# Spectral filter and mixture of experts on one core: small matmuls of the routing placed behind a count or a sum instead of in places of their own

## The chip, the core and the metric

The kernel runs on one core of a Trainium2 chip. Five engines work side by side, each through its own instructions in order: PE (TensorE, matrix products), DVE (VectorE), ACT (ScalarE), POOL (GpSimd, which here issues the indirect DMAs) and SP (SyncE, which issues direct DMAs). The metric is the device time of one execution in microseconds (us), less is better.

## The reference

```python
def _attn_ref(x, filt_r, filt_i):          # x: 8 x 2496 x 256
    X = np.fft.rfft(x, axis=1)
    F = (filt_r + 1j * filt_i)[None, :, :]
    return np.fft.irfft(X * F, n=x.shape[1], axis=1).astype(np.float32)

def _moe_ref(x, w_gate, w1, w2):           # x: 19968 x 256, 8 experts
    cap = N // E                           # 2496 tokens for each expert
    logits = x @ w_gate
    order = np.argsort(-logits.flatten())
...
    for idx in order:
        tok, e = (int(idx) // E, int(idx) % E)
        if assigned[tok] >= 0 or counts[e] >= cap:
            continue
        assigned[tok] = e
        counts[e] += 1
...
    for e in range(E):
        mask = assigned == e
        h = np.maximum(x[mask] @ w1[e], 0.0)
        out[mask] = h @ w2[e]
```

A filter along the sequence by Fourier transforms, then a two-layer network with eight experts. Tokens go to experts greedily, by falling score; an expert that is full takes no more. Every expert ends with exactly 2496 tokens.

## The kernel before

The first 420 us or so hold the Fourier transforms (class `Fft`); their result goes to DRAM as `xs`, and the scores to an array `lg` on chip. The rest is the two-layer network (`Ffn`, the FFN) for one expert slot after the other, with the routing (`Route`) of the next slot woven in.

**The network.** `Ffn.run` takes an expert's 2496 tokens in five tiles of 512 (the last 448). For tile g, `gather` (L819) issues four indirect DMAs on POOL that fetch 128 token rows each into `xg`, by the indices `xid`. `turn` (L826) transposes two of these pieces with four small matmuls (`ptr`, L837), and ACT and DVE copy them as a high and a low part into `xo` and `z`; two turns, half 0 and half 1, make a tile. `first` (L851) does one of eight blocks f of the first layer: six products of 512 columns (`pz`, L859), then ACT and DVE make the high and low part of the result `hl`. The second layer runs by quarters t of a tile: 24 products of 256 columns (`py`, L902), an ACT copy, and a scatter by POOL (L913) to the rows `oid` of the output. `firsts` (L872) yields the blocks, and places the turns of the next tile at blocks 3 and 5 (`TF`), and the gather of the tile after it at block 5. Tile 0 of the next expert is turned by the hook in the last tile's second layer (L1040).

**The search.** For each slot `Route.phase` prepares (L635 to L649: the best open expert of each token, big DVE operations), then searches a score threshold in 11 rounds (`threshold`, L575). A round is a *count* (`counts`, L538: DVE compares all scores with several thresholds, 11 or 13 small 16-bit matmuls at L559 count them, DVE folds the result) and a *sum* (L572: one 16-bit matmul over all partitions), from which DVE makes the next thresholds.

**The look-ups.** When a slot's token set is known, `places` (L745) finds, tile by tile, the rows to fetch and to write. For each tile DVE compares (`GE`, L762), PE runs two *pairs* of 16-bit matmuls (`pr`, L769), ACT counts with a sign function (L773), and DVE ends with `xid` (L779) and `oid` (L786).

**What sets the order.** PE's order is the order in which the program is written (`manual_schedule`); that of DVE, ACT and POOL is made by the framework's scheduler. The class `Pump` writes the routing in between: after each piece of FFN work, `feed(c)` adds the piece's estimated time to a clock. It then steps the look-ups (`side`) if their due time has come, and the search (`main`) while its own has; a step is what stands between two `yield`s, and its kind and size give the next due time by the table `lag`. As long as tile 0 of a slot has no indices, the search stands still (`first`). `until` steps until a tile has its indices; `gather` calls it.

Of the kernel before, what the change touches and what calls it, by code (L numbers as in the profile page):

```python
# [6 lines left out]

F32, F32R = mybir.dt.float32, mybir.dt.float32r
BF, F16, I32 = mybir.dt.bfloat16, mybir.dt.float16, mybir.dt.int32
# [6 lines left out]
G = 22  # L16
# [8 lines left out]
ORD, TF = (1, 0, 0, 1), (3, 5)  # L25
# [108 lines left out]
class Fft:  # L134


    def __init__(s, tc, i, xs, zd, lg, pp):
        s.tc, s.nc, s.i, s.xs, s.zd, s.lg, s.pp = tc, tc.nc, i, xs, zd, lg, pp
        s.zw = s.zo = s.y7 = s.y9 = None
        s.xos = []  # L140
        s.nload = s.nstore = 0
        s.st_x = tc.nc.sync
        s.cps = tc.nc.vector.tensor_copy, tc.nc.scalar.copy
        s.y1c = {}
        s.Y1, s.yt, s.yd, s.z, s.xr, s.vs = {}, {}, {}, {}, {}, {}
# [644 lines left out]
class Ffn:  # L790
# [52 lines left out]
    def run(s, e, pump, hook):  # L843
# [7 lines left out]
        def first(g, f):  # L851
            n = min(512, CAP - 512*g)
            xh, xl = s.xT[e, g]
            p = s.ps.tile([128, 512], F32, name="pz", tag="c", bufs=4)
            m = 0
            for k in range(2):
                sl = slice(1024*k+128*f, 1024*k+128*f+128)
                for w, x in ((w1h, xh), (w1h, xl), (w1l, xh)):
                    nc.tensor.matmul(p[:, :n], w[:, sl], x[:, k, :n], start=m == 0, stop=m == 5)  # L859
                    m += 1  # L860
                yield 0.65 * n / 512
            hl = s.wp.tile([128, 1024], F32R, name="hl", bufs=NH)
            hs.setdefault(g, []).append(hl)
            h, l = (hl[:, 512*k:512*k+512] for k in range(2))
            s.lasta = s.R.relu = nc.scalar.activation(h[:, :n], p[:, :n], AF.Relu).ins  # L865
            if g < 4:
                s.R.low = nc.vector.scalar_tensor_tensor(l[:, :n], p[:, :n], 0.0, h[:, :n].bitcast(F32), op0=OP.max, op1=OP.subtract).ins  # L867
            else:
                for a, b, c in ((384, n, n), (0, 384, 512)):
                    s.R.low = nc.vector.scalar_tensor_tensor(hl[:, c:c+b-a], p[:, a:b], 0.0, h[:, a:b].bitcast(F32), op0=OP.max, op1=OP.subtract).ins  # L870

        def firsts(g, count):  # L872
            for f in range(len(hs.get(g, ())), min(8, len(hs.get(g, ())) + count)):
                if g + 1 < 5:
                    if f == TF[0]:
                        s.turn(e, g + 1, 0)
                    if f == TF[1]:
                        s.turn(e, g + 1, 1)
                        if g + 2 < 5:
                            hook(('g', g + 2))  # L880
                yield from first(g, f)

        hook(('g', 1))
        for g in range(5):
            n = min(512, CAP - 512*g)
            yield from firsts(g, 8)
            if g == 4:
                hook('last')
            if g == 0:
                hook('w2')  # L890
            for t in range(4):
                if g < 4:
                    yield from firsts(g + 1, ORD[t])
# [5 lines left out]
                m = 0  # L899
# [24 lines left out]
def emit(tc, i, out):  # L924
    nc = tc.nc
    with ExitStack() as st:
# [9 lines left out]
        f = Fft(tc, i, xs, zd, lg.rearrange("p (b g) e -> p b g e", g=G), pp)  # L936
# [21 lines left out]
        W = None  # L958
# [19 lines left out]
        pump = Pump(R)  # L978
# [30 lines left out]
        def gather(e, g):  # L1009
            pump.until((e, g))  # L1010
            W.gather(e, g, pump.out[e])
# [11 lines left out]
        def flush(p):  # L1023
            while split and split[0][1] < p:
                with tc.issue_after(W.lasta):
                    W.split(*split.pop(0))
        with tc.manual_schedule(engines={mybir.EngineType.PE}):
            for e in range(8):
                pump.limit = e + 1
                def hook(what):  # L1030
                    if what == 'w2':
                        flush(8)
                    elif isinstance(what, tuple):
                        gather(e, what[1])
                    elif e < 7:
                        if what == 'last':
                            gather(e + 1, 0)
                            flush(4)
                        else:
                            W.turn(e + 1, 0, what - 1)  # L1040
                for pe in W.run(e, pump, hook):
                    pump.feed(pe)
                    n += 1

                    if split and n % PACE == 0:
                        with tc.issue_after(W.lasta):
                            W.split(*split.pop(0))


class Pump:  # L1050
# [3 lines left out]
    def __init__(s, R):  # L1054
        s.R, s.ph, s.tags, s.out, s.limit, s.clock = R, 0, set(), {}, 0, 0.0
        s.main, s.due, s.held = R.phase(0), 0.0, False
        s.side = []
        s.on_w, s.kind = None, ''
        s.lag = dict(d=lambda t: t, G=lambda n: LAGS[s.ph][0] + 0.17 * n, X=lambda n: LAGS[s.ph][1], m=lambda t: 1.0 + 1.2*t, w=lambda t: t,
                     o=lambda t: t, p=lambda t: t, g=lambda t: 3.0)  # L1060

    def step_main(s):
        if s.held:
            if s.ph > s.limit:
                return False
            s.held = False
            tab, BE, widx = s.R.made
            xid, oid = (s.R.wb.tile([128, 20], I32, name=n, bufs=2) for n in ("xid", "oid"))
            s.out[s.ph] = (xid, oid, widx)
            s.side.append([s.clock, s.ph, s.R.places(s.ph, tab, BE, xid, oid)])  # L1070
            s.on_w(s.ph)
            return True
        if s.main is None:
            return False
        y = next(s.main, None)
        if y is None:
            s.ph += 1
            s.main = s.R.phase(s.ph) if s.ph < 8 else None
            return s.main is not None
        k, t = y  # L1080
        s.kind = k
        s.held = k == 'w'
        s.due = s.clock + s.lag[k](t)
        return True
# [5 lines left out]
    def step_side(s, u):  # L1090
        y = next(u[2], None)
        if y is None:
            s.side.remove(u)
            return
        k, t = y
        if k == 'g':
            s.tags.add((u[1], t))
        u[0] = s.clock + s.lag[k](t)

    def feed(s, c):  # L1100
        s.clock += c
        for u in s.side[:1]:
            if u[0] <= s.clock:
                s.step_side(u)
        while s.due <= s.clock and not s.first() and s.step_main():
            pass

    def until(s, tag):
        while tag not in s.tags:
# [23 lines left out]
```

## Time and profile before

| | before |
|---|---|
| median of 3 runs | 1418.15 us (1418.12 to 1419.26) |
| the profiled execution's own time | 1418.68 us |
| its span | 1416.9 us |
| PE busy | 1377.6 us, 97% |
| DVE busy | 891.2 us, 63% |
| ACT busy | 674.6 us, 48% |
| POOL busy | 485.5 us, 34% |
| mean granted clock of PE | 0.989 |

The profile is one execution recorded by the hardware. The span runs from the first to the last instruction; the 1.8 us beside it are start and end. An engine counts as busy while one of its instructions runs; matmuls overlap, so the distance between the starts of two of them tells more than the duration of one. The granted clock is PE's share of full speed: 1.00 is 2.4 GHz, 0.50 is 1.2 GHz.

### The profile page before, as it was taken

The numbers are of one execution on the slowest core, as the hardware profiler recorded it, in microseconds if no ns is written. First come the engines' busy times: TensorE is split into PE (matmuls) and PEld (weight loads), VectorE is DVE, ScalarE is ACT, GpSimd is POOL, SyncE is SP. The second block draws the span as 40 slices with busy tenths as digits, with TensorE's granted clock in tenths as the row PEclk, the third lists the DMA queues.
The fourth block names the chain that finished last, engine by engine and source line by source line (L and its number), as shares of the span: only waits on it lengthen the run. The fifth ranks groups of instructions, "written<-read, shape, count | busy, mean of one in ns | idle before, by whom it ended". The sixth has DMA issues, their size and how long they took to land.

```text
span 1416.9 us, 27230 instructions
## 1 busy us (share of the span) xinstructions
PE 1377.6 (97%) x10338; PEld 1209.3 (85%) x10338; DVE 891.2 (63%) x2548; ACT 674.6 (48%) x1638; POOL 485.5 (34%) x538
## 2 busy tenths in 40 slices
PE   9999999999969999999999999999999999999998
PEld 8998898876437898898888889888898999899988
DVE  5577676775547768668667876876967635423231
ACT  6766666644564346326335534533623635423231
POOL 3343343431023126324421732433334324323312
PEclk9999999999979999999999999999999999999999
DMA  9786675658981022102212212112111321111100
GB/s 374 262 237 184 191 217 137 160 125 239 319 311 57 29 83 70 40 27 97 63 36 75 73 44 83 53 47 99 46 39 49 127 68 51 48 41 51 40 20 29
DMA packets 58700, 153.75 MB, mean 109 GB/s; under 512 B 10953, under 2 KB 32073, under 8 KB 54985
## 3 DMA queue, kind: packets, MB, share of 16 engines
q1 hardware_dynamic: 29920, 70.10, 16.4%
q0 software_dynamic: 18416, 60.37, 13.0%
q10 hardware_dynamic: 10233, 21.53, 4.6%
q8 instruction: 82, 1.34, 0.4%
q14 instruction: 49, 0.40, 0.1%
HBM read 88.32 MB, written 63.70 MB: 107 GB/s over the span
## 4 chain that ended last, share of the span: by engine, by line
PE 58%; issue 5%; DVE 5%; POOL 1%; ACT 1%; DMA 0%; POOLq 0%; DVEq 0%; ACTq 0%
PE py L902 28%; PE pz L859 25%; PE ptr L837 2%; PE rt L559 2%; POOL out L913 1%; PE rt L769 1%; DVE hl L870 1%; DVE w1l L817 1%; DMA wr<-w,widx 0%; DVE tmp L640 0%; DVE Gm L551 0%; DVE hl L867 0%; ACT junka L773 0%; DVE tmp L638 0%; DVE M L636 0%
## 5 line engine op out<-in xcount | busy, mean ns | idle before, releaser
L902 PE MATMUL py<-w1h,hl 128*128 128x256 f32 x2496 | 483.8, 286 | 0.7 <-DVE hl L870 0.7
L902 PEld LDWEIGHTS py<-w1h,hl 128*128 128x128 f32 x2496 | 401.7, 191 | 3.3 <-DVE hl L870 1.1
L902 PE MATMUL py<-w1l,hl 128*128 128x256 f32 (+1 forms) x1280 | 358.8, 282 | 0.0
L913 POOL DMA_INDIRECT out<-y,oid x160 | 167.2, 1045 | 495.8 <-ACT y L912 448.2
L865 ACT ACTIVATE hl<-pz 128x512 fp32r<-128x512 f32 (+1 forms) x320 | 188.0, 588 | 229.6 <-PE pz L859 203.9
L859 PE MATMUL pz<-xo,w0h 128*128 128x512 f32 (+1 forms) x640 | 264.1, 413 | 3.9 <-DVE hl L867 2.1
L867 DVE SCALAR_TENSOR_TENSOR hl<-pz,hl 128x512 fp32r<-128x512 f32 x256 | 175.3, 688 | 135.4 <-ACT hl L865 134.1
L859 PE MATMUL pz<-z,w0h 128*128 128x512 f32 (+1 forms) x640 | 248.6, 388 | 0.0
L859 PE MATMUL pz<-xo,w0l 128*128 128x512 f32 (+1 forms) x640 | 248.4, 388 | 0.0
L902 PEld LDWEIGHTS py<-w1l,hl 128*128 128x128 f32 (+1 forms) x1280 | 241.0, 188 | 1.9
L823 POOL DMA_INDIRECT xg<-xs,xid x160 | 170.6, 1067 | 135.3 <-issue 50.6
L912 ACT COPY y<-py 128x256 f32<-128x256 f32 x152 | 56.6, 372 | 298.7 <-PE py L902 269.5
L859 PEld LDWEIGHTS pz<-xo,w0l 128*128 128x128 f32 x640 | 120.8, 189 | 24.1
L859 PEld LDWEIGHTS pz<-xo,w0h 128*128 128x128 f32 x640 | 121.6, 190 | 22.4 <-DVE hl L867 3.3
L859 PEld LDWEIGHTS pz<-z,w0h 128*128 128x128 f32 x640 | 121.6, 190 | 15.7 <-DVE z L841 0.6
L219 ACT COPY Y<-p 64x240 f32<-64x240 f32 (+1 forms) x302 | 115.3, 382 | 28.6 <-PE p L213 21.1
L237 POOL TENSOR_TENSOR P<-P 128x256 f32<-128x256 f32 x80 | 58.7, 733 | 166.5 <-DVE P L235 166.3
L551 DVE TENSOR_TENSOR Gm<-M,thr 117x1232 bf16<-117x1232 f32 (+2 forms) x80 | 104.4, 1315 | 0.2
L213 PE MATMUL p<-cS,xr 117*128 117x120 f32 x688 | 93.5, 276 | 2.7 <-ACT Y L219 1.5
L213 PEld LDWEIGHTS p<-cS,xr 117*128 117x128 f32 x688 | 85.1, 191 | 6.8 <-ACT Y L219 4.3
L229 PE MATMUL p<-cW,Y 128*128 128x128 f32 x640 | 88.8, 277 | 0.6 <-DVE Q L236 0.6
L229 PEld LDWEIGHTS p<-cW,Y 128*128 128x128 f32 x640 | 80.1, 191 | 5.8 <-issue 3.9
(218 smaller groups left out, 1989.2 us busy)
## 6 DMA issues: line engine op xcount, KB each, us to landing
z<-zd SPq DMA_DIRECT2D x26, 600.0 KB, 5.2
zd<-zt SPq DMA_DIRECT2D x120, 128.0 KB, 3.3
xs<-xo ACTq DMA_DIRECT2D x18, 600.0 KB, 9.8
xr<-x SPq DMA_DIRECT2D x6, 1536.0 KB
xr<-x SPq DMA_DIRECT2D x6, 1216.0 KB, 11.5
zd<-zt ACTq DMA_DIRECT2D x40, 128.0 KB, 2.6
xs<-xo SPq DMA_DIRECT2D x8, 600.0 KB, 6.2
xr<-x SPq DMA_DIRECT2D x8, 512.0 KB, 6.8
```

Of the source, the lines that this page charges most:

```text
L213: s.lastmm = nc.tensor.matmul(p[:, q-q0, :120], xv[:, q-24*h], s.cS1, start=True, stop=True).ins
L219: c = (nc.vector.tensor_copy if (t == 5 if b else cp) else nc.scalar.copy)(dst, src)
L229: nc.tensor.matmul(p[:, k], s.Y1[b][:, 4*g+k, dh*128:dh*128+128], s.cW[:, 4*g+k], start=True, stop=True)
L237: nc.gpsimd.tensor_tensor(P[:, :, :64], P[:, :, :64], P[:, :, 64:], op=OP.subtract)
L551: nc.vector.tensor_tensor(Gm[:, s0:s1, :m], s.M[:, s0:s1].unsqueeze(2).to_broadcast([117, s1 - s0, m]), thr[:117].unsqueeze(1).to_broadcas ...
L823: s.lastg = s.nc.gpsimd.indirect_dma_start(out=xg[:n], out_offset=None, in_=s.xs, in_offset=bass.IndirectOffsetOnAxis(ap=ids[0][:n, t:t+1] ...
L859: nc.tensor.matmul(p[:, :n], w[:, sl], x[:, k, :n], start=m == 0, stop=m == 5)
L865: s.lasta = s.R.relu = nc.scalar.activation(h[:, :n], p[:, :n], AF.Relu).ins
L867: s.R.low = nc.vector.scalar_tensor_tensor(l[:, :n], p[:, :n], 0.0, h[:, :n].bitcast(F32), op0=OP.max, op1=OP.subtract).ins
L902: nc.tensor.matmul(p[:a.stop-a.start], hs[g][f][:, a], b[:, 256*f:256*f+256], start=m == 0, stop=m == 8 * len(terms) - 1, skip_group_check ...
L912: s.lasta = nc.scalar.copy(y, p).ins
L913: st = nc.gpsimd.indirect_dma_start(out=out_rows, out_offset=bass.IndirectOffsetOnAxis(ap=ids[1][:w, 4*g+t:4*g+t+1], axis=0), in_=y[:w], i ...
```

## The change

`firsts` no longer writes a turn into PE's order itself: at blocks 0 and 3 it puts the turn on a list `turns`, and `flush` writes what is still on the list at blocks 3 and 6. So does the hook for tile 0 of the next expert, with a `flush` before the next expert begins. `feed` first steps the search; if one of the steps was a count, a sum or the end of the search (`'G'`, `'X'`, `'m'`), that is a `hit`: one turn of the list is written directly behind it, and then `beside` may write a look-up step behind that. Without a hit, `beside` writes no look-up as long as the search or its preparation runs (`soon`), but for the step behind a finished tile (`'g'`).

```diff
@@ firsts
                 if g + 1 < 5:
-                    if f == TF[0]:
-                        s.turn(e, g + 1, 0)
+                    if f in (0, 3):
+                        pump.flush()
+                        pump.turns.append(partial(s.turn, e, g + 1, f // 3))
+                    if f == 6:
+                        pump.flush()
                     if f == TF[1]:
-                        s.turn(e, g + 1, 1)
                         if g + 2 < 5:
                             hook(('g', g + 2))
@@ hook
                         else:
-                            W.turn(e + 1, 0, what - 1)
+                            pump.flush()
+                            pump.turns.append(partial(W.turn, e + 1, 0, what - 1))
+                pump.flush()
                 for pe in W.run(e, pump, hook):
@@ Pump
-            s.side.append([s.clock, s.ph, s.R.places(s.ph, tab, BE, xid, oid)])
+            s.side.append([s.clock, s.ph, s.R.places(s.ph, tab, BE, xid, oid), ''])
...
-        u[0] = s.clock + s.lag[k](t)
+        u[0], u[3] = s.clock + s.lag[k](t), k
 
     def feed(s, c):
         s.clock += c
+        hit = False
+        while s.due <= s.clock and not s.first():
+            k = s.kind
+            if not s.step_main():
+                break
+            hit |= k in ('G', 'X', 'm')
+        if hit and s.turns:
+            s.turns.pop(0)()
+        s.beside(hit)
+
+    def beside(s, hit):
+        soon = (s.kind in ('G', 'X', 'd') or s.main is None) and not s.first()
         for u in s.side[:1]:
-            if u[0] <= s.clock:
+            if u[0] <= s.clock and (hit or not soon or u[3] == 'g'):
                 s.step_side(u)
-        while s.due <= s.clock and not s.first() and s.step_main():
-            pass
+
+    def flush(s):
+        hit = len(s.turns) > 0
+        while s.turns:
+            s.turns.pop(0)()
+        if hit:
+            s.beside(True)
```

Both kernels have the same 6978 matmuls from the first FFN product on. The maximal runs of other matmuls between FFN products are 285 before and 206 now. Three places follow; a number behind a name tells one buffer from the next, and lines of the changed kernel are up to 3 higher here (a turn is L838, a pair L770, a count L560, a product L860, a gather L824, a scatter L916).

PE at the start of expert 1's FFN in the changed kernel: `GE` is a pair's operand, `Gm` a count's, `xg_7053` and `xg_7055` are the first two pieces of expert 1's tile 1.

```order
L770 MATMUL rt_7040<-dt_6635,GE_6806 128x180
L860 MATMUL pz_7061<-xo_6996,w0h_6628 128x512
L860 MATMUL pz_7061<-z_6997,w0h_6628 128x512
L860 MATMUL pz_7061<-xo_6996,w0l_6629 128x512
L560 MATMUL rt_7065<-A_3753,Gm_3754 48x96
...
L838 MATMUL ptr_7084<-id_4915,xg_7053 128x128 x2
L838 MATMUL ptr_7084<-id_4915,xg_7055 128x128 x2
L860 MATMUL pz_7061<-xo_6996,w0h_6628 128x512
```

The second pair of tile 1's look-up, whose result gives the indices for `xg_7053`, now stands three products and one count ahead of the turn that reads `xg_7053`; before, it stood 36 first-layer and 88 second-layer products and one count ahead.

POOL around the gathers of expert 1's tiles 0 and 1, before (`xg_7105` to `xg_7111` are tile 1; `y` are results on their way out):

```order
L823 DMA xg_6912<-xs_68,xid_6618 128x256
L913 DMA out<-y_6803,oid_5170 19968x256
L913 DMA out<-y_6950,oid_5170 19968x256
L823 DMA xg_7105<-xs_68,xid_6618 128x256
L823 DMA xg_7107<-xs_68,xid_6618 128x256
L823 DMA xg_7109<-xs_68,xid_6618 128x256
L823 DMA xg_7111<-xs_68,xid_6618 128x256
L913 DMA out<-y_7005,oid_5170 19968x256
```

and in the changed kernel (`xg_7053` to `xg_7059` are tile 1):

```order
L824 DMA xg_6887<-xs_68,xid_6624 128x256
L916 DMA out<-y_6802,oid_5170 19968x256
L916 DMA out<-y_6917,oid_5170 19968x256
L916 DMA out<-y_6961,oid_5170 19968x256
L916 DMA out<-y_6993,oid_5170 19968x256
L916 DMA out<-y_7029,oid_5170 19968x256
L824 DMA xg_7053<-xs_68,xid_6624 128x256
L824 DMA xg_7055<-xs_68,xid_6624 128x256
L824 DMA xg_7057<-xs_68,xid_6624 128x256
L824 DMA xg_7059<-xs_68,xid_6624 128x256
L824 DMA xg_7199<-xs_68,xid_6624 128x256
```

Tile 1's gathers moved behind all five results of expert 0's last quarters; before, two stood ahead of them.

PE one round of the search further on, in the changed kernel (`xg_7057`, `xg_7059` are the second half of tile 1):

```order
L560 MATMUL rt_7152<-A_3753,Gm_3754 128x96
L838 MATMUL ptr_7169<-id_4915,xg_7057 128x128 x2
L838 MATMUL ptr_7169<-id_4915,xg_7059 128x128 x2
L770 LDWEIGHTS GE_7125
L770 MATMUL rt_7176<-dt_6635,GE_7125 128x180
...
L770 MATMUL rt_7186<-dt_6635,GE_7125 128x180
L860 MATMUL pz_7207<-xo_6996,w0h_6628 128x512
```

Count, turn and two look-up pairs stand in one row; before, a pair, the count and the turn of this place each had three products between them.

## Rows read from the trace of the kernel before

**Rows 1.** The page's first part: busy us, share of the span, instructions.
```profile
PE 1377.6 (97%) x10338; PEld 1209.3 (85%) x10338; DVE 891.2 (63%) x2548; ACT 674.6 (48%) x1638; POOL 485.5 (34%) x538
```
**Rows 2.** Timeline of PE around a count: start, duration in us, instruction, count.
```profile
699.74 0.28 PE L902 MATMUL py<-w1h,hl 128*128 128x256 f32 x1
699.86 0.57 PE L559 MATMUL rt<-A,Gm 117*128 117x80 bf16 x11
...
700.46 0.28 PE L902 MATMUL py<-w1l,hl 128*128 128x256 f32 x1
...
702.37 0.28 PE L902 MATMUL py<-w1h,hl 128*128 128x256 f32 x1
```
**Rows 3.** Timeline of PE around a single look-up pair.
```profile
652.26 0.28 PE L902 MATMUL py<-w1h,hl 128*128 128x256 f32 x1
652.39 0.33 PE L769 MATMUL rt<-dt,GE 117*128 117x180 f16 x2
...
652.71 0.29 PE L902 MATMUL py<-w1l,hl 128*128 128x256 f32 x1
```
**Rows 4.** Timeline of PE: a turn alone (after 739.48), then count and turn together.
```profile
739.48 0.40 PE L859 MATMUL pz<-xo,w0l 128*128 128x512 f32 x1
...
740.38 0.39 PE L859 MATMUL pz<-z,w0h 128*128 128x512 f32 x1
...
742.67 0.40 PE L859 MATMUL pz<-xo,w0l 128*128 128x512 f32 x1
742.90 0.57 PE L559 MATMUL rt<-A,Gm 117*128 117x80 bf16 x11
743.31 0.63 PE L837 MATMUL ptr<-id,xg 128*128 128x128 f32 x4
...
744.01 0.40 PE L859 MATMUL pz<-z,w0h 128*128 128x512 f32 x1
```
**Rows 5.** Timeline of PE: a look-up pair and a count together.
```profile
802.39 0.28 PE L902 MATMUL py<-w1h,hl 128*128 128x256 f32 x1
802.51 0.33 PE L769 MATMUL rt<-dt,GE 117*128 117x180 f16 x2
802.68 0.48 PE L559 MATMUL rt<-A,Gm 117*128 117x64 bf16 x11
803.00 0.36 PE L902 MATMUL py<-w1h,hl 128*128 128x256 f32 x1
803.20 0.28 PE L902 MATMUL py<-w1l,hl 128*128 128x256 f32 x1
```
**Rows 6.** Timeline of DVE and of POOL behind the pair at 652.39: indices and gathers.
```profile
654.34 0.16 DVE L779 SCALAR_TENSOR_TENSOR xid<-ex,js 128x4 int32<-128x4 f32 x1
...
655.25 0.98 POOL L823 DMA_INDIRECT xg<-xs,xid  x1 [1.93 <-issue]
656.53 0.95 POOL L823 DMA_INDIRECT xg<-xs,xid  x1 [0.30 <-issue]
```
**Rows 7.** DMA issues by line: the last number is the median us to landing.
```profile
xg<-xs,xid POOLq DMA_INDIRECT x160, 2.8
```
**Rows 8.** Stretches (us): length, busy time by engine, PE's granted clock, DMA.
```profile
372.90:376.30 3.40, 1.21 (x8) 0.38 (x5) 0.80 (x3) 0.67 (x2) 0.00 (x0) 1.00 0.85 246
376.30:379.70 3.40, 3.40 (x6) 1.73 (x7) 1.22 (x6) 2.07 (x5) 0.00 (x0) 0.50 0.60 146
...
422.30:427.50 5.20, 5.18 (x12) 3.78 (x13) 4.59 (x6) 1.88 (x4) 3.34 (x3) 0.50 0.73 277
428.30:431.70 3.40, 1.49 (x10) 1.04 (x8) 3.40 (x6) 1.56 (x3) 0.00 (x0) 1.00 0.00 0
```
**Rows 9.** Timeline of PE: a pair with an idle time before it, and its releaser.
```profile
796.94 0.31 PE L769 MATMUL rt<-dt,GE 117*128 117x180 f16 x2 [0.84 <-DVE t L567]
```
**Rows 10.** Timelines of PE and of DVE: tile (1,1)'s second pair and its indices.
```profile
538.83 0.33 PE L769 MATMUL rt<-dt,GE 117*128 117x180 f16 x2
...
548.23 0.15 DVE L779 SCALAR_TENSOR_TENSOR xid<-ex,js 128x4 int32<-128x4 f32 x1
```

More of the change, by code (lines that the diff above doesn't have):

```diff
@@ L6 @@
 from contextlib import ExitStack, nullcontext
+from functools import partial
 F32, F32R = mybir.dt.float32, mybir.dt.float32r
@@ L1056, in __init__ @@
         s.main, s.due, s.held = R.phase(0), 0.0, False
-        s.side = []
+        s.side, s.turns = [], []
         s.on_w, s.kind = None, ''
```

## The prediction, made before the changed kernel ran

> **What bounds the kernel now.** I read the page first, then TensorE's timeline around single look-ups, counts and turns, then the path of a token index from a look-up to a gather, and last the granted clock around TensorE's few long waits. A tile is named by two numbers, (expert, tile), both from 0; a *visit* is a run of look-up, count, sum or turn matmuls between two products of the feed-forward network (FFN).
>
> TensorE is the bound: it is busy for 97% of the span [rows 1], and from about 422 us on it runs FFN products almost without a gap: one every 0.12 us for the second layer (16 from 700.46 to 702.37 [rows 2]), one every 0.23 us for the first (ten from 740.38 to 742.67 [rows 4]). So whatever a visit takes from this stream is paid in full, and so is a wait. A visit's price is the distance between the product before it and the second product behind it, less two spacings; the second, since what a visit leaves behind shows only there. A count alone: 699.74 to 700.46, so 0.72 - 0.24 = 0.48 us [rows 2]. A look-up pair alone: 0.45 - 0.24 = 0.21 us [rows 3]. A turn alone: 0.90 - 0.46 = 0.44 us [rows 4].
>
> **What the change does, part by part.**
>
> *Joints.* The order of before has 285 visits in the FFN stretch, that of the change 206, with the same matmuls in them. 79 pieces thus lose a visit of their own and stand behind another piece. Counting both orders: 59 of these joints have a turn on one side, 20 join a pair to a count or a sum. Two joints that before has by chance give the price. Count and turn together: 742.67 to 744.01, so 1.34 - 0.46 = 0.88 against 0.48 + 0.44 = 0.92: 0.04 us saved [rows 4]. Pair and count together: 802.39 to 803.20, so 0.81 - 0.24 = 0.57 against 0.21 + 0.48 = 0.69: 0.12 saved [rows 5], of which a part is only that this count is 64 columns wide and the other 80. I take 0.04 for joints with a turn and 0.09 for the others: 59 x 0.04 + 20 x 0.09 = **-4.2 us**. Bounds: 79 x 0.04 = 3.2, 79 x 0.12 = 9.5, and 0 if a joined piece has to wait for its operand as often as it saves.
>
> The Trainium skill speaks against any gain here: "TensorE: Matmul & The Clock Gate", section "Step-by-step: what each phase is for", has the next weights loaded while the running matmul streams, so that a visit would cost only its own columns wherever it stands. By that this term would be 0. The trace does not agree for these mixed streams: behind a visit the second product starts 0.20 us after the first, not 0.12 (803.00 and 803.20 [rows 5]).
>
> *Look-ups held back.* With the new rule a pair is issued only with a count or a sum, as long as the search runs or its preparation does. Between two searches there is no count for the whole preparation, so the look-ups of tile 1 of the next expert, done in the preparation before, now stand at its end. In before the pair for (1,1) is at 538.83 [rows 10], far ahead of the turn that needs its tokens; nothing waits. In the change three products and one count stand between them, as the first excerpt of the order shows. TensorE works in its written order, so behind the waiting turn stand the products of (1,0), and behind those, with nothing to do, ACT and DVE.
> How long the path is: the pair starts at 652.39, DVE has the indices at 654.34 + 0.16 = 654.50, POOL issues the first gather at 655.25 and the second at 656.53 [rows 3, 6], and a gather lands 2.8 us after its issue [rows 7]. The turn needs two gathers: 656.53 + 2.8 - 652.39 = 6.9 us from the pair. What TensorE has to do in between: pair 0.21, three products 0.69, count 0.48, first half of the turn 0.2, so 1.6. Wait at (1,1): 6.9 - 1.6 = **5.3 us**. On POOL five scatters instead of two now stand ahead of these gathers, the last of them with the expert's last result; it becomes ready while the indices are made, so I add nothing. If it is late the bound is one more POOL step, 1.28 [rows 6].
> The same sum for the other places of the new order where pair and turn are near: (2,1), 22 + 9 products, a turn and a count between: 0.21 + 2.64 + 0.44 + 2.07 + 0.48 + 0.2 = 6.0, wait **0.9**. (3,2), 24 first-layer products, a sum (counted as nothing) and a count: 6.4, wait **0.5**. (1,2) comes to 7.1 and (3,1) to 7.5: no wait. Everywhere else the distance is over 9 us. Together 6.7; from 5 (indices as early as 2.1 us at each place) to 9 (each 0.5 later).
>
> *The clock behind the long wait.* TensorE was busy for 1.21 of 3.40 us up to 376.3, and the next 3.4 us were granted 0.50, the lower of the two levels [rows 8]. It was busy for 1.49 of 3.40 us up to 431.7, and the clock stayed at 1.00 [rows 8]. A wait of 5.3 us is far longer than the idle time in either, so I count the fall, at the length that the first shows: 3.4 us at 1.2 instead of 2.4 GHz, half of it lost: **+1.7 us**. Bounds: 0, and half of the 5.2 us of dense products that ran at 0.50 after the start of the FFN [rows 8], 2.6.
> The Trainium skill has the same effect in "TensorE: Matmul & The Clock Gate", section "HAM oscillation — how this bites in real kernels": waits for data inside dense matmuls drop the clock. By the rows at 428.30 alone the term would be 0, by that section it is due; no run here shows it inside the FFN.
>
> *Waits that go.* One pair of the preparation waited 0.84 us for DVE [rows 9]; the change issues none there. **-0.8 us.** Bounds 0 and 3.
>
> *Turns.* Half 0 of a turn moves up by as much as three blocks of six products, half 1 stands at the same place or up to one block later (1.4 us). Their gathers, but for the places above, have landed long before, and half 1 still has two blocks, 2.8 us, until its columns are used; I count nothing. ACT and DVE do the same work as before.
>
> **The sum.** -4.2 + 6.7 + 1.7 - 0.8 = +3.4 us. Against the profiled execution's 1418.68 that is 1422.1; the median of the runs is 0.5 lower, so the forecast is **1421.6 us**. A measurement of this kernel can tell about 0.2% from no change, 2.8 us: "the same" is 1415.3 to 1421.0.
>
> **The rivals.**
> *Not slower: joints are worth what the pair shows.* At 0.12 us each they give 9.5 in place of 4.2: 1421.6 - 5.3 = 1416.3. Place: all 79 joints. For it: rows 5. Against: rows 4, and most joints have a turn. It decides from about 0.06 us per joint on, where the sum falls below +2.8. A chance of 0.33.
> *A visit costs only its columns* (the page's first rule as a mechanism here): no joint saves anything, and the waits stay: 1421.6 + 4.2 = 1425.8. For it: two of the measured joints save only hundredths. Against: both save something. 0.08.
> *Indices late at (1,1).* In the new order the last large operation of the preparation stands on DVE directly ahead of this pair's reads. In before such a pair, at 538.83, had its indices only at 548.23 [rows 10], 7.3 us later than the 2.1 counted. If half of that returns, +3.7: 1425.3. Against: in the change the preparation should be over. 0.14.
> *The forecast:* 0.45.
>
> **How the numbers follow.** The forecast's own spread, some 3 us to either side (the joint price and whether the clock falls), lies just over the border of "the same": I give slower 0.28 and same 0.17 of its 0.45. With the two slow rivals slower comes to 0.50. Of the first rival 0.19 is within 0.2% and 0.14 below (clock steady as well: 1414.6). So faster 0.14, same 0.36, slower 0.50. The range leaves out the far ends only: from 1415.0 (dear joints, half of the clock term) to 1428.0 (late indices, cheap joints).
>
> **What would show it.** In the changed profile the list of TensorE's waits should have a new entry, the turn for the gather, of about 5 us in all, near the start of expert 1's products, a second of about 1 us near the start of expert 2's, and a stretch at half clock behind the first. The number of visits falls to 206, and a joined count and turn costs about 0.88 us. Right would be a sum of these near +3. The prediction is wrong if the turn at (1,1) waits under 2 us, if the joints save 0.1 us or more each, or if DVE makes sums wait that did not wait before.

## The result and the profile after

| | before | after |
|---|---|---|
| median of five runs each | 1418.15 us | 1435.53 us (1434.74 to 1436.12) |
| ratio, 95% interval | 1 | 1.0108 (1.0094 to 1.0122) |
| the profiled execution, its span | 1418.68, 1416.9 us | 1434.74, 1433.0 us |
| from the first FFN product to the last | 988.7 us | 1004.3 us |

The change costs 17 us; forecast were 3.4, and the range ended at 1428.0. Nearly all of it lies in the FFN stretch (+15.6 of the 16.1 us between the profiled executions). Not all chips are alike: on three of the five chips used below the kernel before takes 1436 to 1442 us instead of 1418 to 1419, so each ratio is against the kernel before on the same chip, and each experiment names its chip by a letter. Each chip ran one set of experiments only, so what belongs to the chip and what to the hour of the set can't be told apart.

The first part of the page after, which answers to [rows 1]:

```profile
PE 1379.3 (96%) x10338; PEld 1211.9 (85%) x10338; DVE 890.1 (62%) x2548; ACT 676.4 (47%) x1638; POOL 485.0 (34%) x538
```

TensorE does the same work and is busy for 1.7 us longer (1377.6 before); the other 14 of the 16 us are idle time. The list of TensorE's waits after (line waited <- releaser: us in total, times, longest):

```profile
PE ptr L838 <- DMA xg<-xs,xid: 17.8, 7, 11.0
...
PE pz L860 <- ACT xo L841: 4.9, 8, 0.7
PE pz L860 <- DVE hl L868: 4.1, 4, 2.9
PE pz L860 <- DVE z L842: 3.0, 9, 0.9
```

and two lines of the same list of before:

```profile
PE ptr L837 <- DMA xg<-xs,xid: 11.0, 2, 10.7
...
PE pz L859 <- DVE hl L867: 2.1, 2, 1.9
```

The wait of 11 us for a gather is the start of the FFN and stands in both, with a second one of 0.3 to 0.4 us. New are five waits of turns for gathers, 6.5 us together, of a kind that the prediction had; and products that wait for the two copies of a turn, `xo` by ACT and `z` by DVE, 7.9 us together (0.7 of it in before too), which it had not. Seven places hold 6.0 of these 7.9 us. One of them, TensorE, ACT and DVE at the start of expert 3's products, after:

```profile
817.28 0.28 PE L905 MATMUL py<-w1l,hl 128*64 128x256 f32 x1
817.40 0.60 PE L838 MATMUL ptr<-id,xg 128*128 128x128 f32 x4
...
818.03 0.59 ACT L841 CAST xo<-ptr 128x512 fp32r<-128x512 f32 x1
818.65 0.69 DVE L842 TENSOR_TENSOR z<-ptr,xo 128x512 fp32r<-128x512 f32 x1 [0.24 <-ACT xo L841]
818.67 0.49 PE L860 MATMUL pz<-xo,w0h 128*128 128x512 f32 x1 [0.68 <-ACT xo L841]
819.40 0.50 PE L860 MATMUL pz<-z,w0h 128*128 128x512 f32 x1 [0.23 <-DVE z L842]
```

Half 1 of the next expert's tile 0 is written directly ahead of the product that reads it. TensorE is through with it in 0.6 us and then waits for ACT's copy, starts one product, and waits again for DVE's. From 817.28 to the second product at 819.40 are 2.12 us, where a lone turn takes some 0.8 (two spacings, 0.35, and its price, 0.45): 1.3 us lost. In before, 16 second-layer products, together 1.9 us, stood between the same turn and its reader, and nothing waited:

```profile
807.41 0.60 PE L837 MATMUL ptr<-id,xg 128*128 128x128 f32 x4
...
809.72 0.39 PE L859 MATMUL pz<-xo,w0h 128*128 128x512 f32 x1
```

Where the 15.6 us are, from the distances between all products of the two profiled executions. A visit's waiting is its cost less the price of its pieces (a pair 0.20, a sum 0.13, a turn 0.45, a count some 0.4 to 0.6 by its width, as each stands alone), with what a joint saves (below) taken off that price:

| us | forecast | measured |
|---|---|---|
| joints: 15 before, 94 after (a visit may hold several) | -4.2 | -4.1 |
| waits for gathers at (1,1), (1,2), (3,2), (2,1): 4.7, 1.7, 1.4, 0.4 | +6.7 | +8.2 |
| products at half clock behind (1,1) | +1.7 | +1.0 |
| half 1 of the next expert's tile 0 ahead of its readers, 7 places | 0 | +8.8 |
| expert 0's first tile | 0 | +2.9 |
| (1,2)'s visit at 574.5 and a wait at 544.8 | 0 | +1.0 |
| waits of before that are gone, less small new ones | -0.8 | -2.1 |
| sum | +3.4 | +15.7 |

**Joints.** Timeline of TensorE after: count and turn together, then count and pair together.

```profile
703.37 0.39 PE L860 MATMUL pz<-xo,w0l 128*128 128x512 f32 x1
703.60 0.57 PE L560 MATMUL rt<-A,Gm 117*128 117x80 bf16 x11
704.00 0.63 PE L838 MATMUL ptr<-id,xg 128*128 128x128 f32 x4
704.39 0.47 PE L860 MATMUL pz<-xo,w0h 128*128 128x512 f32 x1
704.70 0.39 PE L860 MATMUL pz<-z,w0h 128*128 128x512 f32 x1
```
```profile
842.18 0.28 PE L905 MATMUL py<-w1h,hl 128*128 128x256 f32 x1
842.30 0.50 PE L560 MATMUL rt<-A,Gm 117*128 117x64 bf16 x11
842.63 0.32 PE L770 MATMUL rt<-dt,GE 117*128 117x180 f16 x2
842.74 0.36 PE L905 MATMUL py<-w1h,hl 128*128 128x256 f32 x1
842.94 0.28 PE L905 MATMUL py<-w1l,hl 128*128 128x256 f32 x1
```

The first costs 1.33 - 0.46 = 0.87 us, as in [rows 4]; the second 0.76 - 0.24 = 0.52, where a count of 64 columns alone costs 0.42 and a pair 0.20: 0.10 saved. Behind the joined visit, too, the second product starts 0.20 us (256 columns) or 0.31 us (512) after the first instead of 0.12 and 0.23. These 0.08 us come once for each visit and are of the size of what a visit less saves (0.02 to 0.10); that they are the saving is not shown. The Trainium skill ("TensorE: Matmul & The Clock Gate", section "Step-by-step: what each phase is for") has the next weights load while the running matmul streams; the rule that the prediction drew from it, that a visit costs only its columns, did not hold for this mixed stream.

**(1,1).** TensorE, DVE and POOL after; it answers to [rows 3, 6 and 10].

```profile
557.64 0.32 PE L770 MATMUL rt<-dt,GE 117*128 117x180 f16 x2
...
559.71 0.16 DVE L780 SCALAR_TENSOR_TENSOR xid<-ex,js 128x4 int32<-128x4 f32 x1
559.87 0.65 PE L560 MATMUL rt<-A,Gm 117*48 117x96 bf16 x11
...
560.65 0.99 POOL L824 DMA_INDIRECT xg<-xs,xid  x1 [1.24 <-PE rt L560]
561.94 0.96 POOL L824 DMA_INDIRECT xg<-xs,xid  x1 [0.31 <-issue]
...
563.39 0.44 PE L838 MATMUL ptr<-id,xg 128*128 128x128 f32 x2 [2.88 <-DMA xg<-xs,xid]
...
564.68 0.69 PE L838 MATMUL ptr<-id,xg 128*128 128x128 f32 x2 [0.85 <-DMA xg<-xs,xid]
```

From the pair to the second landing: 564.68 - 557.64 = 7.0 us; forecast was 6.9. The wait comes to 4.7 us; forecast were 5.3. Behind it the stretches that answer to [rows 8] (us, busy by engine, granted clock, DMA):

```profile
560.50:564.20 3.70, 0.46 (x3) 0.20 (x2) 0.67 (x3) 0.00 (x0) 2.89 (x3) 1.00 0.25 71
564.24:567.65 3.41, 2.97 (x8) 2.48 (x9) 1.03 (x2) 1.18 (x2) 0.95 (x1) 0.50 0.26 77
```

TensorE was busy for 0.46 of 3.70 us, and the next 3.4 us were granted 0.50, the level of 1.2 GHz. Dense products are 0.43 us apart there instead of 0.23, and that costs 1.0 us; forecast were 1.7. The section that the prediction set against its rows (the Trainium skill, "TensorE: Matmul & The Clock Gate", section "HAM oscillation — how this bites in real kernels": waits for data among dense matmuls drop the clock) holds here, inside the FFN.

**(1,2)**, where the prediction had no wait, TensorE, DVE and POOL after:

```profile
574.39 0.32 PE L770 MATMUL rt<-dt,GE 117*128 117x180 f16 x2 [0.30 <-DVE loc L771]
...
577.78 0.16 DVE L780 SCALAR_TENSOR_TENSOR xid<-ex,js 128x4 int32<-128x4 f32 x1
578.68 0.94 POOL L824 DMA_INDIRECT xg<-xs,xid  x1 [13.28 <-issue]
579.92 1.53 POOL L824 DMA_INDIRECT xg<-xs,xid  x1 [0.30 <-issue]
...
583.27 0.44 PE L838 MATMUL ptr<-id,xg 128*128 128x128 f32 x2 [1.36 <-DMA xg<-xs,xid]
```

The path takes 8.9 us here, not 6.9: the indices come 3.5 us behind the pair instead of 2.1 [rows 3, 6], since on DVE a block's `hl`, which itself waits 1.0 us for ACT, stands ahead of the last steps to `xid`; and the second gather is there 3.35 us after its issue instead of 2.8.

**Expert 0.** TensorE after, then before:

```profile
432.93 0.50 PE L860 MATMUL pz<-xo,w0h 128*128 128x512 f32 x1 [2.88 <-DVE hl L868]
...
442.97 0.50 PE L860 MATMUL pz<-z,w0h 128*128 128x512 f32 x1 [0.92 <-DVE z L842]
```
```profile
431.64 0.50 PE L859 MATMUL pz<-xo,w0h 128*128 128x512 f32 x1 [1.91 <-DVE hl L867]
```

DVE is behind when the FFN starts, and the first tile's products wait for it longer than before. The wait at 442.97 belongs to a turn inside the expert: half 1 of tile (0,1) is written at 437.54, a block later than before, and DVE copies it only at 442.24, behind a large operation of the preparation (1.43 us). At 440.17 a third product waits, 0.64 us for `hl`.

### The profile page after: what moved, and what is told of

Read it like the earlier page. It is cut to its first block, busy times and chain, and to the rows that moved or that the text cites. A ratio compares the mean times of both kernels' runs of the same rounds, so it can differ in the third digit from the quotient of the medians.

```text
span 1433.0 us, 27178 instructions
## 1 busy us (share of the span) xinstructions
PE 1379.3 (96%) x10338; PEld 1211.9 (85%) x10338; DVE 890.1 (62%) x2548; ACT 676.4 (47%) x1638; POOL 485.0 (34%) x538
## 3 DMA queue, kind: packets, MB, share of 16 engines
q1 hardware_dynamic: 29920, 70.10, 16.1%
q8 instruction: 82, 1.34, 0.4%
## 4 chain that ended last, share of the span: by engine, by line
PE 43%; issue 5%; DVE 1%; POOL 1%; ACT 1%; DMA 0%; POOLq 0%; DVEq 0%; ACTq 0%
PE py L905 20%; PE pz L860 19%; PE ptr L838 2%; POOL out L916 1%; PE rt L560 1%; PE rt L770 1%; DVE z L842 0%; DMA xg<-xs,xid 0%; DVE hl L868 0%; ACT xo L841 0%; ACT hl L866 0%; DVE w0l L818 0%; PE rt L573 0%; ACT junka L774 0%; DVE tmp L641 0%
## 5 line engine op out<-in xcount | busy, mean ns | idle before, releaser
L905 PE MATMUL py<-w1h,hl 128*128 128x256 f32 x2496 | 478.0, 285 | 0.2 <-DVE hl L871 0.2
L916 POOL DMA_INDIRECT out<-y,oid x160 | 170.1, 1063 | 444.2 <-ACT y L915 385.9
L860 PE MATMUL pz<-xo,w0h 128*128 128x512 f32 (+1 forms) x640 | 260.5, 407 | 9.9 <-ACT xo L841 4.9
L860 PE MATMUL pz<-z,w0h 128*128 128x512 f32 (+1 forms) x640 | 250.0, 391 | 3.0 <-DVE z L842 3.0
L860 PE MATMUL pz<-xo,w0l 128*128 128x512 f32 (+1 forms) x640 | 248.8, 389 | 0.0
L824 POOL DMA_INDIRECT xg<-xs,xid x160 | 167.9, 1049 | 201.8 <-PE ptr L838 62.5
L860 PEld LDWEIGHTS pz<-xo,w0h 128*128 128x128 f32 x640 | 121.8, 190 | 32.1 <-ACT xo L841 7.2
L860 PEld LDWEIGHTS pz<-z,w0h 128*128 128x128 f32 x640 | 121.7, 190 | 23.1 <-DVE z L842 6.5
L860 PEld LDWEIGHTS pz<-xo,w0l 128*128 128x128 f32 x640 | 121.0, 189 | 23.4
```

Source lines behind the costliest of these rows:

```text
L824: s.lastg = s.nc.gpsimd.indirect_dma_start(out=xg[:n], out_offset=None, in_=s.xs, in_offset=bass.IndirectOffsetOnAxis(ap=ids[0][:n, t:t+1] ...
L905: nc.tensor.matmul(p[:a.stop-a.start], hs[g][f][:, a], b[:, 256*f:256*f+256], start=m == 0, stop=m == 8 * len(terms) - 1, skip_group_check ...
L916: st = nc.gpsimd.indirect_dma_start(out=out_rows, out_offset=bass.IndirectOffsetOnAxis(ap=ids[1][:w, 4*g+t:4*g+t+1], axis=0), in_=y[:w], i ...
```

## The experiments

The theory after the first reading: two losses, the half 1 ahead of its readers and the gathers, and joints that gain. The rivals: one of the two holds nearly all of it; or the joints cost, by waits for ACT and DVE.

**First set (chip A, before 1442.23 us).** `slot_turns_back` is the change with tile 0 of the next expert turned where it was before:

```diff
-                            pump.flush()
-                            pump.turns.append(partial(W.turn, e + 1, 0, what - 1))
-                pump.flush()
+                            W.turn(e + 1, 0, what - 1)
```


> The change, with the two turns of the next expert's tile 0 written again at the quarters where they stood before; the turns inside an expert and the look-ups as in the change. Theory R (half 1 of that turn now stands directly ahead of the first product that reads it, at seven places, some 1.3 us each): 8 to 10 us faster than the change, near 1426.5, with no idle of TensorE before the first product of an expert. Theory G (only the look-ups that are held back cost anything): within 2 us of the change, 1434. Theory D (joined pieces come to ACT and DVE in bursts, and products wait all over): within 3 us of the change.

`prep_free` lets look-ups be issued during the preparation:

```diff
-        soon = (s.kind in ('G', 'X', 'd') or s.main is None) and not s.first()
+        soon = (s.kind in ('G', 'X') or s.main is None) and not s.first()
```


> The change, with look-ups allowed again during the preparation between two searches (one letter of the rule is taken out); all turns as in the change. Theory G: the waits of turns for gathers at (1,1), (1,2), (2,1) and (3,2) and the half clock behind the first go, 4.8 + 1.7 + 0.5 + 1.4 + 1.6 = 10 us less, less some 1 us for 22 joints undone: near 1426.5. Theory R: within 2 us of the change. Theory D: within 3 us of the change.

`both` has the two edits:

> Both of the edits together: slot turns back, look-ups free in the preparation; 229 visits instead of 285 are left of the change. R and G together: the sum of the two gains, 1416 to 1419, that is what the joints alone bring (56 joints at about 0.05 to 0.09 us, 3 to 5 us under the kernel before, less any new small waits). Theory D: still above 1424.

`slot_turns_late` is the kernel before with only these turns late; `late` writes the turn that was kept:

```diff
...
-                            W.turn(e + 1, 0, what - 1)
+                            late()
+                            late.turn = (e + 1, 0, what - 1)
+                late()
                 for pe in W.run(e, pump, hook):
```


> The kernel before, with one thing of the change alone: half 0 of the next expert's tile 0 is turned one quarter later, half 1 directly before the next expert's first product; no joints, look-ups as before. Theory R: 8 to 10 us slower than before, near 1427. Theories G and D: no difference, 1418.

Measured: 1.0007 (0.9990 to 1.0024), 1.0083 (1.0053 to 1.0113), 1.0024 (1.0004 to 1.0044) and 1.0047 (1.0028 to 1.0067), in this order. Late slot turns alone, without anything else of the change, make the kernel before slower, and the profile of `slot_turns_late` has the mechanism: five of the seven places take the same 2.12 us as in the change, the two others 2.5 and 4.8. But the expectations were in microseconds of a chip like the first, on this chip before itself is 24 us longer, and the change did not run beside these; so the sizes do not decide between the theories.

**Parts of the change (chip B, before 1419.12 us).** `change_again` is the change. `turns_only` keeps the turns inside an expert behind counts and sums, slot turns and look-ups as before; `lookups_only` keeps the new rule for look-ups, all turns as before; `mended` is `both`, with expert 0's turns at their old blocks and the last flush at block 5:

```diff
+                    if e == 0:
+                        if f in TF:
+                            s.turn(e, g + 1, TF.index(f))
...
-                    if f == 6:
+                    if f == TF[1]:
                         pump.flush()
```


> The change itself once more, as the measure for the three that run beside it on the same chip. Every theory: 1.009 to 1.013 of the kernel before.

> Of the change only the turns inside an expert behind a count or a sum; slot turns and look-ups at their own times as before (252 visits for 285). Theory J (a joint of a turn saves what the traces show, 0.04 to 0.1 us, and nothing else moves): 33 joints, 1.3 to 3.3 us faster than before, ratio 0.998 to 0.999. Theory D (the joined pieces load ACT and DVE at once, and sums and products wait for them): ratio 1.002 or more, and the list of waits has DVE before the sum or the product more often than before.

> Of the change only the rule for look-ups, in the preparation too (234 visits for 285); all turns at their places of before, so that pair and turn of tile (1,1) are 4.7 us apart instead of 1.1. Theory J and G: 51 joints save 3 to 5 us, the wait at (1,1) gives back some 2 to 3, ratio 0.998 to 1.001. Theory D: ratio 1.003 or more.

> The version that should keep the gain without the new waits: slot turns as before, look-ups free in the preparation, turns behind a count or a sum for experts 1 to 7 only, and written at block 5 at the latest. 236 visits for 285. Theory J: 49 joints, 2.5 to 4 us faster than before, ratio 0.997 to 0.998. Theory D: 1.001 or more.

| chip B | ratio, 95% interval | prices of all visits, us | all waiting, us |
|---|---|---|---|
| before (the first table's profile, another set) | 1 | 90.6 | 18.4 |
| change_again | 1.0119 (1.0101 to 1.0137) | 86.5 | 38.7 |
| turns_only | 1.0017 (1.0001 to 1.0033) | 88.9 | 21.8 |
| lookups_only | 1.0038 (1.0022 to 1.0054) | 86.6 | 25.8 |
| mended | 0.9998 (0.9989 to 1.0007) | 87.9 | 19.8 |

"All waiting" is what the products' distances have beyond undisturbed spacings and the prices, products at half clock included. Every version saves 1.7 to 4.1 us by its joints, and each but `mended` waits for more than that saves; `mended` comes out even. Of the expectations only that of `change_again` and the rival's for `lookups_only` (1.003 or more) were met: `turns_only` lies between its two theories, and `mended` gained nothing where 0.2 to 0.3% were expected. The look-up rule and the turns inside an expert, each alone, make 0.38 and 0.17%; of the change's 1.19% that leaves some 9 us for the slot turns if the parts add up, beside the 8.8 of the table. In `lookups_only` there are four new waits for gathers (4.7 us), the longest at expert 7. TensorE there, then stretches with the granted clock:

```profile
1300.58 0.52 PE L838 MATMUL ptr<-id,xg 128*128 128x128 f32 x2 [2.83 <-DMA xg<-xs,xid]
1301.59 0.69 PE L838 MATMUL ptr<-id,xg 128*128 128x128 f32 x2 [0.49 <-DMA xg<-xs,xid]
```
```profile
1297.30:1300.70 3.40, 0.57 (x3) 0.17 (x3) 1.21 (x3) 0.60 (x1) 2.48 (x3) 1.00 0.19 51
1300.70:1304.10 3.40, 2.91 (x9) 2.17 (x9) 0.69 (x1) 0.59 (x1) 1.36 (x2) 0.51 0.33 104
1304.10:1307.50 3.40, 3.40 (x20) 2.81 (x20) 1.59 (x5) 2.07 (x5) 0.00 (x0) 0.99 0.00 0
```

A wait behind a held-back look-up again drops the clock for 3.4 us, with the turns at their old places.

**The first set again (chip C, before 1435.88 us).**

> The change with the next expert's tile-0 turns back at their old places, on another chip than slot_turns_back, so that it stands beside a calm kernel before. Theory (two causes that add: half 1 of the next expert's tile 0 directly ahead of its readers, seven times about 1.2 us, and the late gathers with their clock fall, about 8 us): 8 to 9 us less than the change, so 1.005 to 1.007 of the kernel before. Rival (the gathers' waits are nearly all of the loss): 1.010 or more, as the change itself.

> The change with look-ups free to be issued during the preparation, beside the same kernel before. Theory: the waits for gathers at (1,1), (1,2), (2,1), (3,2) and the half-clock stretch go, about 8 us; what stays is the slot turns' 9: 1.005 to 1.008 of before. Rival (slot turns are all): 1.011 or more.

> Both edits together. Theory: both losses go and the joints are left, with a small new wait at expert 0's turn: 0.998 to 1.002 of before, and the two single gains add up to the joint one within 0.2%. Rival (the joints themselves cost, by waits for DVE and ACT): 1.004 or more.

> The kernel before with only the next expert's tile-0 turns late (half 0 a quarter later, half 1 directly before the next expert's first product). Theory: seven waits of about 1.2 us, 1.005 to 1.007 of before. Rival (such a turn costs only in company of the change's other moves): 0.999 to 1.001.

Measured: 1.0008 (0.9995 to 1.0022), 1.0087 (1.0063 to 1.0111), 1.0031 (1.0013 to 1.0049), 1.0042 (1.0024 to 1.0060): as on chip A. The additive theory had `back_again` at 1.005 to 1.007 and `both_again` at most at 1.002, and missed both; `free_again` lies just above its range, and `late_again` just under it. In `late_again`, too, five of the seven places take 2.12 us. On these two chips the look-up rule costs nothing that a ratio shows: without the slot turns the change is even with before.

**The slot turns beside the change (chip D, before 1419.10 us).** `half1_back` moves only half 1 back:

```diff
                             pump.flush()
-                            pump.turns.append(partial(W.turn, e + 1, 0, what - 1))
+                            if what == 1:
+                                pump.turns.append(partial(W.turn, e + 1, 0, 0))
+                            else:
+                                W.turn(e + 1, 0, 1)
```


> The change unchanged, beside the three others of this call. 1.010 to 1.013 of before if it costs the same on every chip; on a chip whose kernel before takes 1436 us or more its waits may be longer, then up to 1.016.

> The change with both tile-0 turns of the next expert at their old places. If the slot turns are most of the loss, at least 0.7% under the change of this same call (near 1.001 to 1.003 of before, as on two other chips); if the gathers' waits are most, at most 0.4% under it.

> The change with half 1 of the next expert's tile 0 written directly by the hook, a quarter of the second layer ahead of its readers; half 0 stays on the list. Theory (half 1 directly ahead of its readers is the missed term, 7 times 1.1 to 1.3 us): as back_third within 0.2%. Rival (the place of half 0, or of the search's steps around it, costs as much): half of the gain or less.

> The kernel before, unchanged, for its profile on the same chip as the other three: ratio 0.999 to 1.001. Its FFN stretch says how much of the others' waits belongs to the chip and how much to their order.

| chip D | median us | ratio, 95% interval | all waiting, us |
|---|---|---|---|
| before_traced | 1418.90 | 0.9995 (0.9985 to 1.0006) | 18.4 |
| change_third | 1435.55 | 1.0107 (1.0091 to 1.0124) | 38.2 |
| back_third | 1431.99 | 1.0090 (1.0073 to 1.0107) | 34.0 |
| half1_back | 1430.37 | 1.0074 (1.0057 to 1.0091) | 33.3 |

Half 1 alone gives as much as both halves, so it is the harmful one. But of the 8.8 us that the seven places cost, only 3.6 to 5.2 come back. `back_third` is 0.2% under `change_third`, where its expectation took at most 0.4% as a sign for the gathers' waits. The profile of `back_third` says where the rest goes. TensorE, DVE and POOL at (1,1), then stretches with the granted clock:

```profile
559.21 0.48 PE L770 MATMUL rt<-dt,GE 117*128 117x180 f16 x4
...
562.28 0.14 DVE L780 SCALAR_TENSOR_TENSOR xid<-ex,js 128x4 int32<-128x4 f32 x1
563.20 0.98 POOL L824 DMA_INDIRECT xg<-xs,xid  x1 [1.53 <-issue]
...
566.00 0.69 PE L838 MATMUL ptr<-id,xg 128*128 128x128 f32 x2 [4.23 <-DMA xg<-xs,xid]
```
```profile
567.30:570.70 3.40, 3.40 (x9) 2.78 (x10) 1.38 (x2) 1.18 (x2) 0.65 (x1) 0.50 0.26 77
570.70:574.10 3.40, 3.40 (x12) 2.36 (x11) 1.75 (x8) 0.64 (x2) 0.00 (x0) 0.63 0.00 0
```

and at the start of expert 2, DVE, then TensorE:

```profile
695.19 1.43 DVE L552 TENSOR_TENSOR Gm<-M,thr 117x1232 bf16<-117x1232 f32 x1
696.54 0.68 DVE L842 TENSOR_TENSOR z<-ptr,xo 128x512 fp32r<-128x512 f32 x1
```
```profile
697.27 0.50 PE L860 MATMUL pz<-z,w0h 128*128 128x512 f32 x1 [0.85 <-DVE z L842]
```

Counted from the first FFN product (424.56 here, 425.25 in `change_third`), (1,1)'s second pair stands where it stood, at 134.7 us (134.8 in `change_third`). But there the two pairs stood 2.5 us apart, each behind a slot turn. Without these turns they have nothing to stand behind and come at once (x4), and the indices follow 3.1 us behind instead of 2.2. So the first gather starts at 138.6 instead of 137.8 us, and the turn ends its wait 0.8 us later, too: the 1.15 us that the slot turn no longer costs at this place have gone into a longer wait for the gather. And behind the longer wait the clock stays low for longer: it is granted at 0.50 from 563.0 to 573.2 us in `back_third`, for 6.8 us in `half1_back` and for 3.4 in `change_third`. The products behind the turn lose some 1.3 us more by that in `back_third` than in `change_third`. At expert 2 half 1 is turned at 693.70, 2.3 us ahead of its reader, and DVE still copies it late, since the compare of a count (1.43 us) stands before the copy in DVE's order.

**The gathers' part beside these (chip E, before 1436.41 us).**

> The change with look-ups free to be issued in the preparation. The profile of change_third has 9.4 us of waits behind late gathers at (1,1), (1,2), (2,1) and (3,2) and about 1.2 us of products at half clock behind the first. Theory (these go, the slot turns' 8.9 us stay): 1.003 to 1.006 of before on a chip whose kernel before takes about 1419 us. Rival (as with the slot turns, a part of each removed wait comes back at the next one): 1.007 or more.

> Both edits. Theory: slot turns' and gathers' waits both go, so that the joints' gain of 5 to 6 us stands against expert 0's 3 us: 0.998 to 1.001 on such a chip. Rival (the rest of the turns on the list costs too): 1.002 or more, as on the two other chips.

Measured: 1.0093 (1.0070 to 1.0116) and 1.0044 (1.0016 to 1.0071): a chip like A and C, so the condition of both expectations was not met, and the price of the gathers' waits alone on a chip like B and D was not measured by taking them out. It rests on the table of the profile, and on `lookups_only`, which has such waits without the slot turns (chip B, +0.38%).

What sets chips A, C and E apart shows in ACT's and DVE's idle time. The groups of ACT's first pass and DVE's second over a first-layer result (line, count | busy us, mean ns | idle before, what ended it) in `late_again` on chip C, then in `before_traced` on chip D:

```profile
L865 ACT ACTIVATE hl<-pz 128x512 fp32r<-128x512 f32 (+1 forms) x320 | 187.9, 588 | 240.8 <-PE pz L859 191.5 <-issue 18.5 <-PE rt L572 10.6
L867 DVE SCALAR_TENSOR_TENSOR hl<-pz,hl 128x512 fp32r<-128x512 f32 x256 | 175.4, 688 | 138.8 <-ACT hl L865 126.1 <-issue 11.3
```
```profile
L865 ACT ACTIVATE hl<-pz 128x512 fp32r<-128x512 f32 (+1 forms) x320 | 187.9, 588 | 229.6 <-PE pz L859 201.8 <-PE rt L572 10.6 <-DVE hl L867 7.1
L867 DVE SCALAR_TENSOR_TENSOR hl<-pz,hl 128x512 fp32r<-128x512 f32 x256 | 175.2, 687 | 135.5 <-ACT hl L865 134.2
```

On chip C, 18.5 and 11.3 us of idle time end with "issue", a wait for nothing that the profile shows; on chip D there are no such waits among the largest. Work of the same duration simply starts late there. The same kernel shows it as well: between 425 and 1405 us the waits of over 0.2 us that end with "issue" come to 20.2 us on ACT and 28.4 on DVE in `back_again` (C), to 2.5 and 0 in `back_third` (D). TensorE itself has 0.5 us of them in `slot_turns_back` and `back_again`, 3.9 to 7.5 in the eight other profiles of A, C and E, 2.6 to 3.9 of it between 449 and 458 us, and in these eight a stretch at half clock begins there. No profile of before was taken on these chips, so it stays open how much of that it has itself, and why the change without its slot turns is even with before there.

## Why the prediction was wrong

- **The step that failed is "Turns".** It said that half 1 stands at the same place or up to a block later and "still has two blocks, 2.8 us, until its columns are used; I count nothing". That is so for the turns inside an expert but for two: tile (0,1)'s half 1 kept a product waiting for 0.9 us (442.97), another for 0.3 (1012.01). For the turns that the hook lists, the flush before the next expert's first product puts half 1 directly ahead of its readers, seven times, and the profile has 8.8 us there. `slot_turns_late` and `late_again` show the mechanism by itself (2.12 us at five places each; +0.4 to 0.5% on A and C, where the size is mixed with waits of the chip); `half1_back` shows that half 1 is the piece (-5.2 us on D). The loss can't be taken out alone: about half of it returns at (1,1), by a longer wait and a longer stretch at half clock, and at (2,0).
- **Waits for gathers: right in kind, and in place but for (1,2); 8.2 us instead of 6.7.** At (1,1) the path came as worked out (7.0 us for 6.9), the wait was 4.7 for 5.3. (1,2), where the text has "no wait", and (3,2) were mis-sized: the sum used one path of 6.9 us everywhere, and at these places it took 8.9 and 7.8, since the indices came 0.4 to 1.4 us later in DVE's order and the second gather landed 0.4 to 0.55 us later. The text gave "each 0.5 later" as the bound; it was up to 2.
- **The clock fell where it was said to**, for the 3.4 us that it was said to, at 1.0 us instead of 1.7, since a part of the stretch fell on the end of the wait and on the turn. The length is not fixed: the same program had 6.8 us at half clock there on chip B (`change_again`, from 559.6, half of it in the wait), 3.4 on chip D.
- **Joints: right, -4.1 against -4.2.** The rival by which they are worth 0.12 each, and the one by which they are worth nothing, both fall.
- **Waits that go: larger than thought (-2.1), and eaten by expert 0's start (+2.9)**, which no step had. Its first wait is 0.6 to 1.0 us longer than before in every variant of the change on B and D, also with the turns of expert 0 at their old blocks (`mended`); what makes DVE later there stays open. The wait at 442.97 is gone in `mended`.
- **The rival "indices late at (1,1)"** did not occur: 2.2 us from the pair to the indices.
- Of what it named as signs against itself two did not happen (the turn at (1,1) waited 2.88 + 0.85 = 3.7 us, not under 2; the joints saved 0.04 us on average). The third did, but at no cost that matters: two sums waited for DVE, 0.3 us together, where the list of before has none. The signs covered the terms that it had; none covered the one it lacked.

How the 17 us split between slot turns and gathers is shown by the profile's waits and not by undoing: the waits follow each other on TensorE, and taking out one lengthens the next.

## What to carry to other kernels

When an instruction is put on a list to be written "at the next good moment", look at the latest moment, the flush: what stands behind it there, and does that read it? On an engine that runs in written order, a producer directly ahead of its reader costs the whole chain through the other engines, here 1.1 to 1.4 us a time, whatever the joining saves (0.02 to 0.10 us). And holding a look-up back to save it a place of its own pays only where its reader on TensorE stands further off than the chain from look-up to reader is long, here 7 to 9 us.

## What was not expected of the hardware

- The second of four gathers took 1.53 us to issue at 579.92, and 1.34 at 832.72, where [rows 6] have 0.95; the turns that wait for these two start 3.35 and 3.2 us after the issue, not 2.8 [rows 7].
- The same edit costs different amounts on different chips: the change without its slot turns is 1.0090 on chip D and 1.0008 on C (there before is 17 us longer itself).
- The same program stayed at half clock behind the wait at (1,1) for 3.4 us on chip D and 6.8 on chip B; `back_third`, with a wait of 4.23 instead of 2.89 us there, for 10.2.
